# Two sets of small f32 buffers for the Strassen-like units, and two subtractions moved to VectorE, in a fused pooled-attention and SiLU-MLP kernel

## The chip, the cores and the metric

The kernel runs on one core of one Trainium2 chip. The metric is the device time of one execution in microseconds. Beside it stands a profile of one execution, whose span (first to last instruction) is about 2 us shorter than the time.

## The reference

Attention with keys and values pooled over 8 positions, then a two-layer MLP with SiLU over all tokens:

```python
k_p = k.reshape(B, H, Sp, pool, D).mean(axis=3)      # B, H, S, D = 8, 8, 576, 64; pool = 8, Sp = 72
v_p = v.reshape(B, H, Sp, pool, D).mean(axis=3)
scores = scale * np.matmul(q, k_p.transpose(0, 1, 3, 2))
attn = softmax(scores)
x = (attn @ v_p).transpose(0, 2, 1, 3).reshape(4608, 512)
h = x @ w_in                                          # 512 -> 2048
out = (h * sigmoid(h)) @ w_out                        # 2048 -> 512, float32
```

## The kernel before

The 4608 tokens are worked in nine tiles of 512 (`t` = 0 to 8). While tile `t` goes through the MLP, the attention of batch `t + 1` (576 tokens) is computed between its matmuls, so that its output `xT` is there for the tiles that follow. An order written out by hand sets what stands behind what on each engine; no scheduler moves it. Tiles 0 to 2 use a list of "fillers" with due places (`up`, `down`, `down_quarters`). Tiles 3 to 8 use `run`, which walks through the string `PROGRAM`, one token at a time.

**Matrix products in seven parts.** Most of both MLP products is done in Strassen's way: a 2x2 block product takes seven block products instead of eight, in return for sums before and after. In the first layer a *unit* is a set of four 128-row groups of the hidden layer; there are four unit sets, A, B, C, E (numbers 0, 1, 2, 3). The seven products of a unit go into three PSUM banks P, Q, R, which later products add to:

- product 2 into P, then ScalarE copies P to `r_sb` (line 506);
- product 5 into Q, then VectorE: `rr_sb` = Q + `r_sb` (line 509);
- product 1 into R, then VectorE: `t_sb` = R - `rr_sb` (line 512);
- product 4 added to P and 3 to Q, and ScalarE's SiLU of each into `h_T`;
- product 7 added to P, VectorE: `c_sb[0]` = P + `t_sb` (line 521), and 6 added to Q, VectorE: `c_sb[1]` = Q + `t_sb` (line 524), and SiLU of both (tokens `h` or `a`, and `s`).

A token such as `E3` in `PROGRAM` means product 3 of unit set E. An addition to a bank must come after what reads the bank's earlier contents: E3 adds to Q, so it waits for the addition that makes `rr_sb` of E from Q. Each product of a unit is four matmuls of 256 columns. The four unit sets are interleaved in the order C, B, A, E, each starting before the one before it has ended, and all of them use the one `r_sb`, the one `rr_sb` and the one `t_sb`.

**The second layer** (`down_stages`, tokens `d40` to `d63`) is one more product in seven parts over halves of `h_T`; five of its left-hand sides are sums `h_sum` (line 610, tokens such as `h6l`: sum number 6, low half; `h6h`, high half). It uses the same `r_sb`, `rr_sb` and `t_sb`. Two corrections are tokens of their own, on GpSimd (POOL):

- `u1`: `rr_sb` -= `o_sb[1]` left half (after product 2 has been copied there);
- `u2`: `rr_sb` -= `o_sb[0]` right half (after product 5 has been copied there).

Then `t_sb` = R + `rr_sb` (line 727) and the two last outputs (lines 729 and 733), each followed by its store. In the last tile, the end of `PROGRAM` is replaced by `L0` and `L1`: products 1, 7 and 6 are done for column half 0 with their additions and stores, and then for column half 1 (`columns`), so that less is left after the last matmul.

**Attention.** `scores` computes a visit's scores for a third of a batch and ScalarE's exponentials into `es`; `denominators` sums them with a matmul and makes the reciprocal `rec` by a logarithm into `lnd` and an exponential; `numerators` multiplies with the pooled values and writes `xT`. The third visit's numerators come in the next tile (token `npp`), except for the last batch. These small tiles come from a pool that hands out its buffers in turn; a new user of a buffer waits for the last reader of the one before.

Of the kernel before, what the change touches and what calls it, by code (L numbers as in the profile page):

```python
# [27 lines left out]
FP32 = mybir.dt.float32  # L28
FP32R = mybir.dt.float32r
BF16 = mybir.dt.bfloat16  # L30
# [6 lines left out]
def kernel(  # L37
# [9 lines left out]
    nc = tc.nc  # L47
# [3 lines left out]
    SP = S // POOL  # L51
# [9 lines left out]
    KQ, NQ, CQ = KG // 2, NTT // 2, d_model // 2  # L61
# [8 lines left out]
    VW = max(HS, 2 * S // 3)  # L70
# [11 lines left out]
    singles = ctx.enter_context(tc.tile_pool(name="singles", bufs=1))  # L82
    big = ctx.enter_context(tc.tile_pool(name="big", bufs=1))
    mid = ctx.enter_context(tc.tile_pool(name="mid", bufs=2))
# [22 lines left out]
        n: singles.tile([128, KQ, NQ], BF16, name=f"h_sum{n}") for n in (1, 2, 5, 6, 7)  # L107
    }
    o_sb = [singles.tile([128, 2, d_model], FP32, name=f"o_sb{n}") for n in range(2)]
    r_sb = singles.tile([128, 2, CQ], FP32, name="r_sb")  # L110
    rr_sb = singles.tile([128, 2, CQ], FP32, name="rr_sb")
    t_sb = singles.tile([128, 2, CQ], FP32, name="t_sb")
    xT = singles.tile([128, KF, NX], BF16, name="xT")

    w_sum1 = [
# [217 lines left out]
    def scores(b, segs):  # L333
        st = batches[b]
        w = width(segs)
        sc = [ps_tile([128, 512], FP32, "at", "sc_ps")[:SP, :w] for s in range(4)]
        for g, i0, i1, cs in seg_cols(segs):
            for c in range(2):
                for s in range(4):
                    rows = slice(32 * s, 32 * (s + 1))  # L340
                    nc.tensor.matmul(  # L341
                        sc[s][:, cs],
                        lhsT=kz[b % 2][rows, g, c, :],
                        rhs=st["qT"][rows, g, i0:i1, :, c],
                        start=(c == 0), stop=(c == 1),
                    )
        es = mid.tile([SP, 4, VW], BF16, tag="es", bufs=4, name="es")[:, :, :w]
        for s in range(4):
            nc.scalar.activation(es[:, s, :], sc[s], func=AF.Exp, scale=score_scale)  # L349
        st["es", segs] = es  # L350


    def denominators(b, segs, on_dve=False):
        st = batches[b]
        w = width(segs)
        es = st["es", segs]
        den_ps = ps_tile([128, 512], FP32, "at", "den_ps")
        for s in range(4):
            nc.tensor.matmul(  # L359
                den_ps[32 * s : 32 * (s + 1), :w],  # L360
                lhsT=ones, rhs=es[:, s, :], start=True, stop=True,
            )
        rec = mid.tile([128, VW], FP32, tag="rec", bufs=4, name="rec")[:, :w]
        if on_dve:
            nc.vector.reciprocal(rec, den_ps[:, :w])
        else:
            lnd = mid.tile([128, VW], FP32, tag="lnd", name="lnd")[:, :w]
            nc.scalar.activation(lnd, den_ps[:, :w], func=AF.Ln)  # L368
            nc.scalar.activation(rec, lnd, func=AF.Exp, scale=-1.0)
        st["rec", segs] = rec  # L370
# [107 lines left out]
    def unit_stages(t, step):  # L478
        ps = {}

        def product(y, n, bank, first):
            if first:
                tag = "mm" if bank == "R" else "at"
                ps[y, bank] = ps_tile([128, 2, NQ], FP32, tag, f"u_ps{bank}")
            w, x = unit_weights(y, n), unit_x(t, n)
            for u in range(2):
                next(step)
                for kk in range(2):
                    nc.tensor.matmul(  # L489
                        ps[y, bank][:, u, :], lhsT=w[:, kk, 128 * u : 128 * (u + 1)],  # L490
                        rhs=x[:, kk, :], start=first and u == 0 and kk == 0,
                        stop=kk == 1, skip_group_check=True,
                    )

        def hidden(y, i, j, src):
            g = UNITS[y][i]
            nc.scalar.activation(  # L497
                h_T[:, g : g + 2, j * NQ : (j + 1) * NQ], src, func=AF.Silu
            )

        tt = nc.vector.tensor_tensor

        def stage(y, n):
            if n == "2":
                product(y, 2, "P", True)
                nc.scalar.copy(r_sb, ps[y, "P"])  # L506
            elif n == "5":
                product(y, 5, "Q", True)
                tt(out=rr_sb, in0=ps[y, "Q"], in1=r_sb, op=ALU.add)  # L509
            elif n == "1":  # L510
                product(y, 1, "R", True)
                tt(out=t_sb, in0=ps[y, "R"], in1=rr_sb, op=ALU.subtract)  # L512
            elif n == "4":
                product(y, 4, "P", False)
                hidden(y, 1, 0, ps[y, "P"])
            elif n == "3":
                product(y, 3, "Q", False)
                hidden(y, 0, 1, ps[y, "Q"])
            elif n == "7":
                product(y, 7, "P", False)  # L520
                tt(out=c_sb[0], in0=ps[y, "P"], in1=t_sb, op=ALU.add)  # L521
            elif n == "6":
                product(y, 6, "Q", False)
                tt(out=c_sb[1], in0=ps[y, "Q"], in1=t_sb, op=ALU.add)  # L524
            elif n == "h":
                hidden(y, 0, 0, c_sb[0])
            else:
                hidden(y, 1, 1, c_sb[1])

        return stage  # L530
# [106 lines left out]
    def down_quarters(t, fillers, last=False):  # L637
        step = spread(fillers, 7 * 2 * KQ)
        ps = {
            n: ps_tile([128, 2, CQ], FP32, "mm", f"o_ps{n}") for n in "PQR"  # L640
        }
        bank = {2: "P", 5: "Q", 1: "R", 4: "P", 3: "Q", 7: "P", 6: "Q"}
        begun = set()

        def product(n, k0, k1, cs=(0, 1)):
            b = bank[n]
            for kt in range(k0, k1):
                for c in cs:
                    next(step)
                    nc.tensor.matmul(  # L650
                        ps[b][:, c, :], lhsT=left(n, kt, c), rhs=W_OUT[n][:, kt, :],
                        start=b not in begun,
                        stop=kt == k1 - 1, skip_group_check=True,
                    )
                    begun.add(b)

        add, sub = ALU.add, ALU.subtract
        tt = nc.vector.tensor_tensor
        KA = KQ // 2
        product(2, KA, KQ)  # L660
        product(5, KA, KQ)
        product(2, 0, KA)
        nc.scalar.copy(r_sb, ps["P"])
        product(5, 0, KA)
        tt(out=rr_sb, in0=ps["Q"], in1=r_sb, op=add)
        for cc in ((0,), (1,)) if last else ((0, 1),):
            cs = slice(cc[0], cc[-1] + 1)
            product(1, 0, KQ, cc)
            tt(out=t_sb[:, cs], in0=ps["R"][:, cs], in1=rr_sb[:, cs], op=sub)
            product(4, 0, KQ, cc)  # L670
            nc.scalar.copy(o_sb[1][:, cs, LO], ps["P"][:, cs])
            tail = last and cc == (1,)
            if tail:
                store(t, 3, LO, (nc.gpsimd,))
            product(3, 0, KQ, cc)
            nc.vector.tensor_copy(out=o_sb[0][:, cs, HI], in_=ps["Q"][:, cs])
            if tail:
                store(t, 1, HI)
            product(7, 0, KQ, cc)
            tt(out=o_sb[0][:, cs, LO], in0=ps["P"][:, cs], in1=t_sb[:, cs], op=add)  # L680
            for c in cc:
                store(t, c, LO if tail else FULL, (nc.scalar if tail else nc.sync,))
            product(6, 0, KQ, cc)
            tt(out=o_sb[1][:, cs, HI], in0=ps["Q"][:, cs], in1=t_sb[:, cs], op=add)
            for c in cc:
                if tail:
                    store(t, 3, HI, both)
                else:
                    store(t, 2 + c, FULL, (nc.gpsimd if last else nc.sync,))
        for _ in step:  # L690
            pass


    def down_stages(t, last):
        ps = {}
        bank = {2: "P", 5: "Q", 1: "R", 4: "P", 3: "Q", 7: "P", 6: "Q"}
        begun = set()
        add, sub = ALU.add, ALU.subtract
        tt = nc.vector.tensor_tensor

# [39 lines left out]
        def part_of(tok):  # L740
            if tok == "o":
                return after(6)
            n = int(tok[1])
            if tok[0] == "u":
                src = o_sb[1][:, :, LO] if n == 1 else o_sb[0][:, :, HI]
                nc.gpsimd.tensor_tensor(out=rr_sb, in0=rr_sb, in1=src, op=sub)  # L746
                return
            if not ps:
                for b in "PQR":
# [1 line left out]
            i = int(tok[2])  # L751
# [20 lines left out]
    def run(t):  # L772
# [7 lines left out]
        if last:  # L780
            i = toks.index("d10")
            sums = [x for x in toks[i:] if x[0] in "hu"]
            toks = toks[:i] + sums + ["L0", "L1"]
        toks = [x for x in toks if attn or x not in attn_toks]
        if a == B - 1:
            toks.insert(1 + max(toks.index("de2"), toks.index("nu1"), toks.index("o")), "nu2")
# [311 lines left out]
```

## Time and profile before

Time: 280.79 us, median of 3 runs (280.5 to 281.09). The profiled execution's span is 278.9 us; the granted TensorE clock was 0.999 of full speed.

| engine | busy us | share of the span |
|---|---|---|
| TensorE, matmuls (PE) | 271.2 | 97% |
| TensorE, weight loads (PEld) | 208.9 | 75% |
| VectorE (DVE) | 242.5 | 87% |
| ScalarE (ACT) | 190.8 | 68% |
| GpSimd (POOL) | 117.8 | 42% |

Rows of the page that touch the change, in the page's words: `L509 DVE TENSOR_TENSOR rr_sb<-u_psQ,r_sb` x29, 690 ns each; `L512 DVE TENSOR_TENSOR t_sb<-u_psR,rr_sb` x29, 687 ns; `L506 ACT COPY r_sb<-u_psP` x29, 585 ns; `L746 POOL TENSOR_TENSOR rr_sb<-rr_sb,o_sb` x12, 1709 ns; `L349 ACT ACTIVATE es<-sc_ps` x100, 471 ns.

How to read the lines: the first time is microseconds from the start of the span, the second a duration. "out<-in" names what is written and read, and "x4" means that four equal instructions are merged. Brackets at the end give how long the engine had been idle before, and what ended that wait. Matmuls overlap: four of them show 0.60 us, but the next four start 0.44 us after their start. In a table by windows the columns are the length of the window, busy time and count of PE, PEld, DVE, ACT and POOL, the granted clock, the DMA share and GB/s. The chain of waits follows the work that ended last back from the last instruction, and lists it in order of time; "issue" in it is time for which the profile shows no wait.

### The profile page before, as it was taken

The numbers are of one execution on the slowest core, as the hardware profiler recorded it, in microseconds if no ns is written. First come the engines' busy times: TensorE is split into PE (matmuls) and PEld (weight loads), VectorE is DVE, ScalarE is ACT, GpSimd is POOL, SyncE is SP. The second block draws the span as 40 slices with busy tenths as digits, with TensorE's granted clock in tenths as the row PEclk, the third lists the DMA queues.
The fourth block names the chain that finished last, engine by engine and source line by source line (L and its number), as shares of the span: only waits on it lengthen the run. The fifth ranks groups of instructions, "written<-read, shape, count | busy, mean of one in ns | idle before, by whom it ended". The sixth has DMA issues, their size and how long they took to land.

```text
span 278.9 us, 7359 instructions
## 1 busy us (share of the span) xinstructions
PE 271.2 (97%) x2923; PEld 208.9 (75%) x2933; DVE 242.5 (87%) x449; ACT 190.8 (68%) x373; POOL 117.8 (42%) x116
## 2 busy tenths in 40 slices
PE   8999999999999999999999999999999999999975
PEld 4458444576878678887888788877887788888864
DVE  4985777788998979998999899989999889998993
ACT  1788766468677956878677977797779858308700
POOL 8745217242158331945394429972811300130050
PEclk9999999999999999999999999999999999999999
DMA  7999999896759798569757825799510041014013
GB/s 214 280 257 242 206 324 179 237 161 120 159 73 229 196 139 161 140 161 129 134 112 191 133 43 131 184 104 144 138 26 0 2 114 40 2 31 121 1 38 115
DMA packets 31314, 37.73 MB, mean 135 GB/s; under 512 B 10352, under 2 KB 22256, under 8 KB 31280
## 3 DMA queue, kind: packets, MB, share of 16 engines
q0 software_dynamic: 23920, 27.03, 52.5%
q1 hardware_dynamic: 6928, 9.58, 12.5%
q10 hardware_dynamic: 432, 0.66, 0.7%
q8 instruction: 23, 0.38, 0.6%
q14 instruction: 11, 0.09, 0.1%
HBM read 36.70 MB, written 9.44 MB: 165 GB/s over the span
## 4 chain that ended last, share of the span: by engine, by line
PE 73%; DMA 12%; DVE 8%; issue 3%; POOL 2%; DVEq 0%; POOLq 0%
PE o_psQ L705 11%; PE o_psP L705 11%; PE u_psP L489 10%; PE u_psQ L489 9%; DMA w_in_sb<-in_moe_w_in_dram 6%; DMA w_out_sb<-in_moe_w_out_dram 6%; PE o_psQ L650 4%; PE o_psP L650 4%; PE hp_ps L542 4%; PE u_psR L489 4%; PE o_psR L705 4%; DVE t_sb L512 3%; PE sc_ps L341 3%; PE nu_ps L385 3%; PE o_ps L577 2%
## 5 line engine op out<-in xcount | busy, mean ns | idle before, releaser
L610 DVE TENSOR_TENSOR h_sum<-h_T 128x1024 bf16<-128x1024 bf16 (+1 forms) x78 | 57.4, 789 | 1.6 <-ACT h_T L548 1.0
L489 PEld LDWEIGHTS <-w_sum 128*128 128x128 bf16 x532 | 52.0, 98 | 7.2 <-issue 0.3
L705 PEld LDWEIGHTS <-h_sum 128*128 128x128 bf16 x480 | 45.6, 98 | 10.0 <-issue 2.3
L349 ACT ACTIVATE es<-sc_ps 72x384 bf16<-72x384 f32 (+1 forms) x100 | 39.1, 471 | 5.7 <-PE sc_ps L341 5.3
L497 ACT ACTIVATE h_T<-c_sb 128x512 bf16<-128x512 f32 x58 | 35.6, 627 | 8.7 <-DVE c_sb L521 8.4
L746 POOL TENSOR_TENSOR rr_sb<-rr_sb,o_sb 128x512 f32<-128x512 f32 x12 | 20.5, 1709 | 42.0 <-ACT o_sb L719 38.6
L506 ACT COPY r_sb<-u_psP 128x512 f32<-128x512 f32 x29 | 17.0, 585 | 22.6 <-PE u_psP L489 13.4
L542 PE MATMUL hp_ps<-xT,w_in_sb 128*128 128x512 bf16 (+2 forms) x151 | 25.9, 318 | 0.3
L489 PEld LDWEIGHTS <-w_in_sb 128*128 128x128 bf16 x232 | 22.5, 98 | 4.2 <-issue 1.3
L394 DVE TENSOR_TENSOR xT<-nu_ps,rec 128x384 bf16<-128x384 f32 (+1 forms) x50 | 23.9, 530 | 1.6 <-PE nu_ps L385 1.4
L509 DVE TENSOR_TENSOR rr_sb<-u_psQ,r_sb 128x512 f32<-128x512 f32 x29 | 20.0, 690 | 4.5 <-ACT r_sb L506 1.7
L191 POOL TENSOR_TENSOR raw<-raw 72x1024 f32<-72x1024 f32 x10 | 23.6, 2364 | 0.1
L512 DVE TENSOR_TENSOR t_sb<-u_psR,rr_sb 128x512 f32<-128x512 f32 x29 | 19.9, 687 | 3.0 <-PE u_psR L489 0.5
L548 ACT ACTIVATE h_T<-hp_ps 128x512 bf16<-128x512 f32 (+2 forms) x39 | 18.1, 476 | 5.8 <-PE hp_ps L542 4.8
L521 DVE TENSOR_TENSOR c_sb<-u_psP,t_sb 128x512 f32<-128x512 f32 x29 | 19.8, 683 | 1.9 <-PE u_psP L489 1.2
L524 DVE TENSOR_TENSOR c_sb<-u_psQ,t_sb 128x512 f32<-128x512 f32 x29 | 19.8, 684 | 1.3 <-PE u_psQ L489 1.1
L542 PEld LDWEIGHTS <-w_in_sb 128*128 128x128 bf16 x156 | 14.6, 98 | 8.5 <-issue 0.7
L705 PEld LDWEIGHTS <-h_T 128*128 128x128 bf16 x192 | 18.8, 98 | 2.2
L497 ACT ACTIVATE h_T<-u_psQ 128x512 bf16<-128x512 f32 x29 | 17.1, 590 | 3.3 <-PE u_psQ L489 3.1
L497 ACT ACTIVATE h_T<-u_psP 128x512 bf16<-128x512 f32 x29 | 17.4, 599 | 2.2 <-PE u_psP L489 2.1
L368 ACT ACTIVATE lnd<-den_ps 128x384 f32<-128x384 f32 (+1 forms) x23 | 11.2, 487 | 11.0 <-PE den_ps L359 11.0
L489 PE MATMUL u_psQ<-x_sum,w_in_sb 128*128 128x256 bf16 x116 | 17.5, 272 | 0.3
(104 smaller groups left out, 560.2 us busy)
## 6 DMA issues: line engine op xcount, KB each, us to landing
out_dram<-o_sb SPq DMA_DIRECT2D x128, 64.0 KB, 1.9
raw<-in_k_dram POOLq DMA_DIRECT2D x10, 576.0 KB, 8.0
raw<-in_v_dram POOLq DMA_DIRECT2D x10, 576.0 KB, 8.0
q_bf<-in_q_dram POOLq DMA_DIRECT2D x6, 576.0 KB, 10.7
w_in_sb<-in_moe_w_in_dram POOLq DMA_DIRECT2D x8, 256.0 KB, 8.3
w_out_sb<-in_moe_w_out_dram POOLq DMA_DIRECT2D x4, 512.0 KB, 13.5
raw<-in_v_dram POOLq DMA_DIRECT2D x2, 768.0 KB, 11.1
raw<-in_k_dram POOLq DMA_DIRECT2D x1, 768.0 KB, 10.2
```

The lines of the kernel that those rows point to most:

```text
L191: nc.gpsimd.tensor_add(out=raw[:, :, : 2 * D], in0=raw[:, :, : 2 * D], in1=raw[:, :, 2 * D :])
L349: nc.scalar.activation(es[:, s, :], sc[s], func=AF.Exp, scale=score_scale)
L394: nc.vector.tensor_mul(out=xT[:, 2 * g0 + c : 2 * (g0 + ng - 1) + c + 1 : 2, cols], in0=nu[c][:, :w].rearrange("r (g n) -> r g n", g=ng), ...
L489: nc.tensor.matmul(ps[y, bank][:, u, :], lhsT=w[:, kk, 128 * u : 128 * (u + 1)], rhs=x[:, kk, :], start=first and u == 0 and kk == 0, stop ...
L497: nc.scalar.activation(h_T[:, g : g + 2, j * NQ : (j + 1) * NQ], src, func=AF.Silu)
L509: tt(out=rr_sb, in0=ps[y, "Q"], in1=r_sb, op=ALU.add)
L512: tt(out=t_sb, in0=ps[y, "R"], in1=rr_sb, op=ALU.subtract)
L542: nc.tensor.matmul(hp_ps[:, r0:r1], lhsT=w_in_sb[:, kk, g * 128 : (g + 1) * 128], rhs=xT[:, kk, x0 : x0 + r1 - r0], start=(kk == 0), stop= ...
L610: nc.vector.tensor_tensor(out=h_sum[n][:, ks, :], in0=quarter(*a, ks), in1=quarter(*b, ks), op=op)
L650: nc.tensor.matmul(ps[b][:, c, :], lhsT=left(n, kt, c), rhs=W_OUT[n][:, kt, :], start=b not in begun, stop=kt == k1 - 1, skip_group_check= ...
L705: nc.tensor.matmul(ps[b][:, c, :], lhsT=left(n, kt, c), rhs=W_OUT[n][:, kt, :], start=b not in begun, stop=kt == k1 - 1, skip_group_check= ...
L746: nc.gpsimd.tensor_tensor(out=rr_sb, in0=rr_sb, in1=src, op=sub)
```

## The change

Units take turns with two sets of `r_sb`, `rr_sb` and `t_sb`, so that a unit's first sums need not wait until the unit before has read its own; the second layer uses set 0. The 6144 bytes a partition for this come from one buffer fewer of `es` (3 in place of 4), `rec` (3 in place of 4) and `lnd` (1 in place of 2). In the last tile the subtractions `u1` and `u2` go from GpSimd to VectorE, and stand behind the sums `h6h` and `h6l` in its order (before: `u1 h6h h6l u2` over the two engines; after: `h6h h6l u1 u2`, all on VectorE), so that these sums don't meet GpSimd's work.

The line with `r_sbs[0]` below stands once in `down_quarters` and once in `down_stages`.

```diff
-    r_sb = singles.tile([128, 2, CQ], FP32, name="r_sb")
-    rr_sb = singles.tile([128, 2, CQ], FP32, name="rr_sb")
-    t_sb = singles.tile([128, 2, CQ], FP32, name="t_sb")
+    r_sbs = [singles.tile([128, 2, CQ], FP32, name=f"r_sb{n}") for n in range(2)]
+    rr_sbs = [singles.tile([128, 2, CQ], FP32, name=f"rr_sb{n}") for n in range(2)]
+    t_sbs = [singles.tile([128, 2, CQ], FP32, name=f"t_sb{n}") for n in range(2)]
...
-        es = mid.tile([SP, 4, VW], BF16, tag="es", bufs=4, name="es")[:, :, :w]
+        es = mid.tile([SP, 4, VW], BF16, tag="es", bufs=3, name="es")[:, :, :w]
...
-        rec = mid.tile([128, VW], FP32, tag="rec", bufs=4, name="rec")[:, :w]
+        rec = mid.tile([128, VW], FP32, tag="rec", bufs=3, name="rec")[:, :w]
...
-            lnd = mid.tile([128, VW], FP32, tag="lnd", name="lnd")[:, :w]
+            lnd = mid.tile([128, VW], FP32, tag="lnd", bufs=1, name="lnd")[:, :w]
...
         def stage(y, n):
+            r_sb, rr_sb, t_sb = r_sbs[y % 2], rr_sbs[y % 2], t_sbs[y % 2]
...
+        r_sb, rr_sb, t_sb = r_sbs[0], rr_sbs[0], t_sbs[0]
...
                 src = o_sb[1][:, :, LO] if n == 1 else o_sb[0][:, :, HI]
-                nc.gpsimd.tensor_tensor(out=rr_sb, in0=rr_sb, in1=src, op=sub)
+                (nc.vector if last else nc.gpsimd).tensor_tensor(
+                    out=rr_sb, in0=rr_sb, in1=src, op=sub
+                )
...
             sums = [x for x in toks[i:] if x[0] in "hu"]
-            toks = toks[:i] + sums + ["L0", "L1"]
+            toks = toks[:i] + sorted(sums) + ["L0", "L1"]
```

More of the change, by code (lines that the diff above doesn't have):

```diff
@@ L697, in down_stages @@
         begun = set()
+        r_sb, rr_sb, t_sb = r_sbs[0], rr_sbs[0], t_sbs[0]
         add, sub = ALU.add, ALU.subtract
```

## The prediction, made before the change was run

> **What bounds the kernel now.** I read the page first, then busy time by windows, then the chain of waits in order of time for one unit stage, the timeline of VectorE and TensorE there, and last the timeline of the end.
>
> ```profile
> PE 271.2 (97%) x2923; PEld 208.9 (75%) x2933; DVE 242.5 (87%) x449; ACT 190.8 (68%) x373; POOL 117.8 (42%) x116
> 139.00:167.70 28.70, 28.65 (x339) 23.81 (x338) 26.52 (x47) 22.66 (x44) 15.36 (x12) 1.00 0.60 121
> 261.50:278.90 17.40, 12.62 (x114) 10.80 (x112) 12.78 (x21) 2.87 (x6) 4.13 (x4) 0.98 0.17 61
> ```
>
> The second and third lines are windows: length, then busy time of PE, PEld, DVE, ACT and POOL. In a middle tile TensorE is busy 28.65 of 28.70 us: only a hole in TensorE's row is worth anything there. At the end it is busy 12.62 of 17.40 us.
>
> TensorE's holes in tiles 3 to 8 show in the chain of waits. One unit stage, tile 8, in order of time (start, length, what):
>
> ```profile
> 254.96 0.45 PE u_psP L489 x4
> 255.42 0.70 DVE t_sb L512
> ...
> 257.45 0.69 DVE c_sb L524
> ...
> 258.24 0.70 DVE t_sb L512
> ...
> 259.07 0.70 DVE rr_sb L509
> 259.77 0.04 issue
> 259.81 0.60 PE u_psQ L489 x4
> ```
>
> The end leaves TensorE at 254.96, runs through VectorE's additions, and comes back at 259.81. The timeline shows what TensorE loses:
>
> ```profile
> 259.16 0.60 PE L489 MATMUL u_psQ<-x_sum,w_sum 128*128 128x256 bf16 x4
> 259.81 0.60 PE L489 MATMUL u_psQ<-x_sum,w_in_sb 128*128 128x256 bf16 x4
> 259.81 0.31 PEld L489 LDWEIGHTS <-w_in_sb 128*128 128x128 bf16 x3 [0.22 <-issue]
> ```
>
> Four matmuls start 0.44 us after the four before (258.72, 259.16), but E3 starts 0.65 later: a hole of 0.21 us. E3 adds to bank Q of unit set E, so it waits until `rr_sb` of E has read that bank (end of the 259.07 addition). The same step at 119.96, 148.62, 177.28, 205.94 and 235.15 in the chain makes six holes, 1.28 us. I find no other hole in the unit stages of these tiles except the short ones at changes of matmul shape, which wait for no vector.
>
> Why VectorE is late: its 128x512 f32 additions start 0.60 us apart when nothing orders them (256.25, 256.86, 257.45) and 0.79 to 0.83 apart when the later one needs the earlier one finished (257.45 to 258.24, 258.24 to 259.07). The 258.24 addition writes the `t_sb` that 257.45 reads; the 259.07 addition writes the `rr_sb` that 258.24 reads. Neither needs the other's value.
>
> The end of the last tile, timeline:
>
> ```profile
> 268.60 2.96 POOL L746 TENSOR_TENSOR rr_sb<-rr_sb,o_sb 128x512 f32<-128x512 f32 x2
> 268.74 0.69 DVE L723 COPY o_sb<-o_psQ 128x512 f32<-128x512 f32 x1 [0.16 <-PE o_psQ L705]
> 269.35 2.76 DVE L610 TENSOR_TENSOR h_sum<-h_T 128x1024 bf16<-128x1024 bf16 x2
> 269.41 1.04 PE L705 MATMUL o_psP<-w_sum,h_sum 128*128 128x256 bf16 x8
> 272.03 0.41 DVE L727 TENSOR_TENSOR t_sb<-o_psR,rr_sb 128x256 f32<-128x256 f32 x1
> 272.17 1.05 PE L705 MATMUL o_psQ<-w_sum,h_sum 128*128 128x256 bf16 x8 [1.72 <-DVE h_sum L610]
> 273.05 1.04 PE L705 MATMUL o_psR<-w_sum,h_sum 128*128 128x256 bf16 x8
> 275.87 0.42 DVE L733 TENSOR_TENSOR o_sb<-o_psQ,t_sb 128x256 f32<-128x256 f32 x1 [0.45 <-PE o_psQ L705]
> ```
>
> Two h sums take 2.76 us where four took 2.49 at 263.09, and product 6 waits for them.
>
> [...] POOL's subtractions run 268.60 to 271.56, and the pair of h sums ends only 0.55 us after that.
>
> **Part 1, fewer `es`, `rec`, `lnd`: nothing.** It pays for the new buffers: 3072 + 1536 + 1536 bytes a partition freed, 3 x 2048 used. Three exponential tiles are live at most: the third visit's are read by `npp` or its like before the next batch's third visit writes, and a slot comes round to the same visit of the next batch, a tile (28.7 us) later. In the first batch the fourth `scores` reuses a slot whose numerators stand before it in TensorE's own order. `lnd` is written and read by ScalarE alone, with other activations between two uses. High end: one exponential of 0.47 us held in each of five batches, 2.4 us; kept as a rival.
>
> **Part 2, two sets in the units.** Order is C, B, A, E, so neighbours get different sets (C, A: 0; B, E: 1), as does E against the tail (0). No instruction is added. Waits removed: `t_sb` write after the neighbour's c sums, `rr_sb` write after the neighbour's `t_sb`, and ScalarE's copy into `r_sb` after the neighbour's `rr_sb` addition (9.0 us in 13 waits by the page of waits; TensorE shows no hole for it). I rework tile 8, spacing 0.60 us, and at least 0.10 us after the matmuls' end (C6: 253.92 + 0.60, its addition 254.63):
> - t of B: 254.63 + 0.60 = 255.23 (was 255.42).
> - rr of A: A5 ends 255.83, so 255.93 (was 256.25).
> - c sums of B: 256.53; B6 ends 257.14, so 257.25.
> - t of A: 257.85. rr of E: E5 ends 258.45, so 258.55, ending 259.24.
> E3 could go at 259.60 and is free at 259.29. The hole closes with 0.31 us to spare, and even half the saving would close it. The next waits follow by the same step: E6 waits for a ScalarE activation that itself starts on E3's end, and the h sums are ready over 1 us before their product (263.78 against 264.94). So 6 x 0.21 = **1.28 us**. Tiles 1 and 2 have unit stages too, but their only comparable hole (62.20, some 0.17 us) waits for a ScalarE activation: nothing.
>
> **Part 3, the last tile.** It removes two POOL subtractions (1.28 and 1.60 us) and adds two to VectorE, behind the h sums. Relative to the old times:
> - Without POOL the h sums start 269.35 and 269.95 (0.60 apart, as at 263.09) and end at 270.64, so product 6 starts at 270.70 in place of 272.17.
> - The subtractions: the nearest row is the f32 SBUF addition of 128x512 in line 264, 676 ns, whose next, dependent one starts 0.72 us later (24.67, 25.39). Low end 0.68 (7.37, 8.05), high end 0.83, the dependent spacing of line 512. At 0.72: 270.55, 271.27, and `t_sb` at 271.99, ending 272.40. That is where it was (272.03): what the h sums gain, the subtractions take.
> - Queued behind: `t_sb`, and the R matmuls of column 1. In the trace the first matmul of each column-1 product carries a wait for VectorE, by its place for the reading of column 0 from the same bank. So R goes at 272.46, not at 270.70 + 0.87 = 271.57. Then P and Q at 0.875 each: 273.33 and 274.21. Last addition at + 1.07: 275.28, against 275.87.
> Gain **0.59 us**; at 0.68 it is 0.67, at 0.83 it is 0.37. The last store follows as before. POOL's own subtractions were on no other path in this tile.
>
> Sum: 280.79 - 1.28 - 0.59 = 278.92, say **278.9 us**.
>
> **The rivals.**
> - Column-1 matmuls do not wait for column 0's addition: then TensorE is the bound, products at 271.57, 272.45, 273.32, last addition 274.39, 1.48 us gained: 280.79 - 1.28 - 1.48 = 278.0. Against: those waits are in the trace.
> - The tail gives nothing, because subtractions on VectorE cost more than their 0.72: 279.5. For: `t_sb` has only 0.04 us in hand at my price.
> - The holes stay, another wait in place of `rr_sb` (bank Q or ScalarE): only the tail, 280.2. Against: E5 and `r_sb` of E (257.61) are ready before.
> - Slower: three exponential buffers hold `scores` in five batches, 2.4 us, less at most what is gained: 280.79 + 2.4 - 1.88 = 281.3. Against: the order of uses above.
>
> **How the numbers follow.** Forecast 0.66, full tail 0.08, no tail 0.10, holes stay 0.10, slower 0.06. The range 277.9 to 279.9 takes in the first three, 0.84, with the spread of the times before (0.3 us either way). Faster means below 280.23: the first three and half of the fourth, 0.89; same 0.05 from the fourth and a little of the last, 0.06; slower 0.05.
>
> **What would show it.** Right: E3 0.44 us after A6, the product in front of it, in every tile; ScalarE's `r_sb` no longer waiting for `rr_sb`; pairs of `c_sb` and `t_sb` 0.60 apart; in the last tile two h sums in about 1.3 us, and product 6 after a wait near 0.4 in place of 1.72, then a new hole near 0.9 before R. Wrong: the hole of 0.21 still there, ScalarE's `es` waiting for numerators, or `t_sb` of the last tile well past 272.

## The result and the profile after

The changed kernel takes 279.25 us (median of 6 runs, 279.04 to 279.42) against 280.99 for the kernel before, measured again beside it (median of 6, 280.5 to 281.7). The ratio is 0.9936 [0.9922, 0.995]: 1.74 us faster. The profiled spans are 277.0 us after and 278.9 before.

From the page of the kernel after, busy time by engine and the shares of the chain that ended last:

```profile
PE 270.7 (98%) x2923; PEld 209.1 (75%) x2933; DVE 241.2 (87%) x451; ACT 191.3 (69%) x373; POOL 114.3 (41%) x114
PE 82%; DMA 12%; POOL 2%; DVE 1%; issue 1%; DVEq 0%; POOLq 0%
```

VectorE has two instructions more (449 to 451) and GpSimd two fewer (116 to 114): the two subtractions. VectorE's share of the chain was 8% before (`PE 73%; DMA 12%; DVE 8%; issue 3%` on its page) and is now 1%: the chain no longer leaves TensorE for VectorE in front of E3.

The unit stage of tile 8, timeline of the kernel after. It runs 1.19 us earlier than before:

```profile
255.36 0.68 DVE L522 TENSOR_TENSOR c_sb<-u_psP,t_sb 128x512 f32<-128x512 f32 x1
...
256.06 0.69 DVE L525 TENSOR_TENSOR c_sb<-u_psQ,t_sb 128x512 f32<-128x512 f32 x1
...
256.67 0.68 DVE L513 TENSOR_TENSOR t_sb<-u_psR,rr_sb 128x512 f32<-128x512 f32 x1
...
257.37 0.69 DVE L510 TENSOR_TENSOR rr_sb<-u_psQ,r_sb 128x512 f32<-128x512 f32 x1
...
257.97 0.60 PE L489 MATMUL u_psQ<-x_sum,w_sum 128*128 128x256 bf16 x4
...
258.41 0.60 PE L489 MATMUL u_psQ<-x_sum,w_in_sb 128*128 128x256 bf16 x4
```

The reader is to see the last two lines: E3 (258.41) starts 0.44 us behind the product in front of it, where it was 0.65. The bank's reader is done well before: the addition that makes `rr_sb` of E ends at 258.06 (257.37 + 0.69), 0.35 us before E3. The `c_sb` to `t_sb` step is 0.61 (256.06 to 256.67), where it was 0.79. The same 0.43 or 0.44 stands in front of E3 in tiles 3 to 7 (at 119.60, 148.05, 176.50, 204.95 and 233.96 us). In the page of waits the 9.0 us of ScalarE's `r_sb` behind VectorE's `rr_sb` are gone.

The end of the last tile, timeline of the kernel after:

```profile
267.95 1.28 DVE L611 TENSOR_TENSOR h_sum<-h_T 128x1024 bf16<-128x1024 bf16 x2
...
269.15 1.41 DVE L749 TENSOR_TENSOR rr_sb<-rr_sb,o_sb 128x512 f32<-128x512 f32 x2
...
269.29 1.05 PE L708 MATMUL o_psQ<-w_sum,h_sum 128*128 128x256 bf16 x8 [0.24 <-DVE h_sum L611]
270.67 0.42 DVE L730 TENSOR_TENSOR t_sb<-o_psR,rr_sb 128x256 f32<-128x256 f32 x1
271.15 1.03 PE L708 MATMUL o_psR<-w_sum,h_sum 128*128 128x256 bf16 x8 [0.81 <-DVE t_sb L730]
...
273.96 0.42 DVE L736 TENSOR_TENSOR o_sb<-o_psQ,t_sb 128x256 f32<-128x256 f32 x1 [0.45 <-PE o_psQ L708]
```

The two h sums take 1.28 us in place of 2.76. Product 6 (269.29) waited 0.24 by the bracket in place of 1.72. A wait that was not there before now stands in front of R of column half 1 (271.15). From the start of R of column half 0 to the start of the last addition it was 7.33 us before (268.54 to 275.87), and is 6.82 now (267.14 to 273.96): 0.51 us gained. This stretch is called the tail below.

How the span's 1.9 us divide: the place of equal matmuls in the two traces moves from 0.15 us early (at 42.4 us, behind the last wait for a load in tile 0) to 1.40 early behind the last hole, in six steps of about 0.21, which makes 1.25; the tail gives 0.51; the 0.15 is the start of the kernel, where tile 0 waits for loads. In the traces below this start lies between 0.15 us earlier and 0.58 later than in the kernel before, so differences of medians below some 0.2 us are not read.

### The profile page after: what moved, and what is told of

Read it like the earlier page. It is cut to its first block, busy times and chain, and to the rows that moved or that the text cites. A ratio compares the mean times of both kernels' runs of the same rounds, so it can differ in the third digit from the quotient of the medians.

```text
span 277.0 us, 7372 instructions
## 1 busy us (share of the span) xinstructions
PE 270.7 (98%) x2923; PEld 209.1 (75%) x2933; DVE 241.2 (87%) x451; ACT 191.3 (69%) x373; POOL 114.3 (41%) x114
## 4 chain that ended last, share of the span: by engine, by line
PE 82%; DMA 12%; POOL 2%; DVE 1%; issue 1%; DVEq 0%; POOLq 0%
PE u_psP L489 14%; PE u_psQ L489 14%; PE o_psP L708 11%; PE o_psQ L708 11%; DMA w_in_sb<-in_moe_w_in_dram 7%; DMA w_out_sb<-in_moe_w_out_dram 6%; PE u_psR L489 5%; PE o_psQ L652 4%; PE o_psP L652 4%; PE o_psR L708 4%; PE hp_ps L543 4%; PE sc_ps L341 3%; PE nu_ps L385 3%; PE o_ps L578 2%; PE den_ps L359 2%; PE o_psR L652 1%
## 5 line engine op out<-in xcount | busy, mean ns | idle before, releaser
L611 DVE TENSOR_TENSOR h_sum<-h_T 128x1024 bf16<-128x1024 bf16 (+1 forms) x78 | 55.7, 765 | 1.8 <-ACT h_T L549 1.0
L749 POOL TENSOR_TENSOR rr_sb<-rr_sb,o_sb 128x512 f32<-128x512 f32 x10 | 16.9, 1687 | 42.3 <-ACT o_sb L722 36.5
L489 PE MATMUL u_psP<-x_sum,w_in_sb 128*128 128x256 bf16 x116 | 17.6, 273 | 0.0
```

Source lines behind the costliest of these rows:

```text
L489: nc.tensor.matmul(ps[y, bank][:, u, :], lhsT=w[:, kk, 128 * u : 128 * (u + 1)], rhs=x[:, kk, :], start=first and u == 0 and kk == 0, stop ...
L611: nc.vector.tensor_tensor(out=h_sum[n][:, ks, :], in0=quarter(*a, ks), in1=quarter(*b, ks), op=op)
```

## The experiments

**The theory**: six holes in front of E3 come from `rr_sb` and `t_sb` being shared by neighbouring units; two sets close them (1.28 us); the moved subtractions shorten the tail by about half a microsecond, because R of column half 1 stays behind `t_sb`; the smaller pools cost nothing. **Rivals**: the whole gain is the tail, or the smaller pools cost something, or it is ScalarE's wait for `rr_sb` (9.0 us) whose removal pays, or the order of the sums and not the engine of the subtractions.

### One half at a time

*The two sets without the tail* (`sets_only`): the change, with the subtractions on GpSimd and in the old order.

```diff
-                (nc.vector if last else nc.gpsimd).tensor_tensor(
-                    out=rr_sb, in0=rr_sb, in1=src, op=sub
-                )
+                nc.gpsimd.tensor_tensor(out=rr_sb, in0=rr_sb, in1=src, op=sub)
...
-            toks = toks[:i] + sorted(sums) + ["L0", "L1"]
+            toks = toks[:i] + sums + ["L0", "L1"]
```

> Two sets and fewer buffers, the last tile's subtractions on GpSimd in the old order. Theory (the holes before E3 are one part of the gain, the end another, and they add): 1.28 us less than the kernel before, ratio 0.9954; no hole before E3 in tiles 3 to 8, and product 6 of column half 0 still waits 1.7 us in the last tile. Rival (the two parts hide each other: with the holes gone the end waits for something that does not move): under 0.6 us less.

Measured: 279.73 us against 280.81, ratio 0.9957 [0.9942, 0.9971], 1.08 us gained. None of the six holes is left; product 6 waits 1.72 us, as before.

*The tail without the sets* (`tail_only`): the kernel before with those two hunks the other way round.

> The last tile's subtractions on VectorE behind the h sums, everything else as before. Theory: 0.5 to 0.6 us less than before, ratio 0.998; the six holes of 0.21 us stay, and the last tile shows a wait of some 0.3 us before product 6 and of 0.8 us before the second R. Rival (the end is worth more on its own, TensorE not being held by column half 0): 1.4 us less.

Measured: 280.35 us, ratio 0.9983 [0.9976, 0.9991], 0.46 us gained. All six holes are there (in tile 8, 259.10 to 259.75), and the tail is the same 6.82 us as with the whole change (268.48 to 275.30). The parts add: 1.08 + 0.46 = 1.54 us against 1.74, with intervals of about 0.4 us on the first and the last.

*The smaller pools alone* (`fewer_bufs`): the kernel before with `es` 3, `rec` 3 and `lnd` 1.

> Only es 3, rec 3 and lnd 1 buffers; one set, old end. Theory: the same time as before, within 0.2%, and no wait of es, rec or lnd for an older reader. Rival (some of the change's gain is eaten by scores that wait for a buffer): 0.3 to 2.4 us more.

Measured: 281.33 us, ratio 1.0019 [1.0012, 1.0025]: 0.52 us slower, which the theory did not have. Nothing waits for a buffer: ScalarE's `es` waits for scores 8 times, 5.3 us in all, in both kernels. What differs is one addition in tile 7, timeline of `fewer_bufs`, VectorE and then TensorE:

```profile
231.21 0.69 DVE L512 TENSOR_TENSOR t_sb<-u_psR,rr_sb 128x512 f32<-128x512 f32 x1
232.39 0.69 DVE L509 TENSOR_TENSOR rr_sb<-u_psQ,r_sb 128x512 f32<-128x512 f32 x1 [0.48 <-ACT h_T L497]
```

```profile
235.04 0.60 PE L489 MATMUL u_psQ<-x_sum,w_sum 128*128 128x256 bf16 x4
235.95 0.60 PE L489 MATMUL u_psQ<-x_sum,w_in_sb 128*128 128x256 bf16 x4 [0.31 <-DVE rr_sb L509]
```

`rr_sb` of A starts 1.18 us behind the addition in front of it, where it was 0.83 before (230.76, 231.59). The hole in front of E3 grows from 0.21 to 0.47 us (0.91 less the 0.44 of four matmuls). With 0.09 lost two products earlier, TensorE loses 0.35 us here. The name in the bracket misleads: nothing that the addition reads or overwrites was late. In VectorE's row (its instructions in order, waits among them) the wait in front of the addition stands at 231.94, 0.45 us before the start, against 0.10 in the kernel before (231.49 to 231.59). The remaining 0.17 us of the median lies within the spread of the start; whether the fewer buffers move the start too is not shown.

*The subtractions before the sums, both on VectorE* (`u_first`): the change with `sorted(sums)` replaced by `sums`, so `u1 h6h h6l u2`.

> The change with the last tile's tokens in the old order u1, h6h, h6l, u2, all on VectorE. Theory (what counts is that GpSimd no longer works beside the h sums, not that the subtractions stand behind them): as fast as the change, to 0.2 us less, because the h sums fill the gap between the two dependent subtractions; product 6 starts 0.6 us later, but R of column half 1, which waits for t_sb, does not. Rival (the order is what pays): 0.5 us more than the change.

Measured: 279.28 us, ratio 0.994 [0.9928, 0.9952], the same as the change. Product 6 starts 0.60 us later within the tail (2.75 us behind R of half 0, against 2.15), and still the last addition comes 0.13 us sooner (6.69 us against 6.82, 267.54 to 274.23): product 6 has time to spare, since R behind it waits for `t_sb` in either order (`t_sb` ends at 271.36 and R starts at 271.42; in the change 271.09 and 271.15). What pays is the engine, not the order.

### Which of the three buffers

Each is `sets_only` with one buffer alternating and the other two shared; for `only_rr`:

```diff
-            r_sb, rr_sb, t_sb = r_sbs[y % 2], rr_sbs[y % 2], t_sbs[y % 2]
+            r_sb, rr_sb, t_sb = r_sbs[0], rr_sbs[y % 2], t_sbs[0]
```

> Of the three buffers only r_sb has two, the end as before. Theory (VectorE's spacing sets E3; ScalarE's wait for r_sb is off the path): the six holes of 0.21 us stay, time as before; ScalarE no longer waits for rr_sb. Rival (the wait of ScalarE's copy into r_sb delays the chain): the holes close, 1.3 us less.

> Only rr_sb has two, the end as before. Theory: VectorE gains about 0.2 us twice between the t of B and the rr of E; more than the hole, so the six holes close and the time is 1.28 us less, as with all three. Rival (the pairs are needed together): holes of 0.1 us or more stay, under 0.7 us less.

> Only t_sb has two, the end as before. Theory: VectorE gains about 0.2 us twice (t of B, t of A), more than the hole, so the six holes close, 1.28 us less. Rival (the pairs are needed together, or rr_sb alone counts): holes stay, under 0.7 us less.

| kernel | us (before: 280.9) | ratio | step to E3 in tile 8 |
|---|---|---|---|
| `only_r` | 281.37 | 1.0018 [1.0011, 1.0024] | 0.65 |
| `only_rr` | 279.71 | 0.9955 [0.994, 0.9969] | 0.43 |
| `only_t` | 279.89 | 0.9962 [0.9948, 0.9977] | 0.44 |

The last column, in the timeline of `only_rr`:

```profile
258.48 0.60 PE L489 MATMUL u_psQ<-x_sum,w_sum 128*128 128x256 bf16 x4
258.91 0.60 PE L489 MATMUL u_psQ<-x_sum,w_in_sb 128*128 128x256 bf16 x4
```

Two `r_sb` alone take ScalarE's waits for `rr_sb` away and gain nothing; the kernel is as slow as `fewer_bufs`, whose pools it has. Two `rr_sb`, or two `t_sb`, close the holes alone: either takes two waits of about 0.2 us each out of VectorE's row in front of E3 (those of `rr_sb` of A and E, or those of `t_sb` of B and A), and the hole was 0.21. In tile 8, from the addition in front of `t_sb` of B to `rr_sb` of E, VectorE takes 4.44 us in the kernel before (254.63 to 259.07), 4.02 in `only_rr`, 4.04 in `only_t`, and 3.93 with all three buffers doubled. In tile 7 0.04 us of the hole stays with two `rr_sb` alone. With two `t_sb` alone one hole of 0.17 us stays, in tile 7 (234.07 to 234.68), where the addition that starts late in `fewer_bufs` has no slack left to hide in.

### What made the smaller pools cost something

> Of the fewer buffers only es 3 and lnd 1; rec keeps four. VectorE then has as many instructions as in the kernel before. Theory (fewer buffers cost nothing by themselves; the 0.35 us lost in tile 7 come from one more wait instruction in VectorE's row, which puts the rr_sb addition of unit A at place 576, a multiple of 64): no late start in tile 7, hole before E3 there 0.21 us, and at least 0.35 us less than with all three cut. Rival (the buffers themselves cost it): the hole of 0.47 us in tile 7 stays.

`es_lnd` is the kernel before with `es` 3 and `lnd` 1, and `rec` left at 4. Measured: 280.83 us, ratio 0.9994 [0.9985, 1.0003]. Its timeline of VectorE in tile 7 shows the step of before, 0.82:

```profile
230.74 0.69 DVE L512 TENSOR_TENSOR t_sb<-u_psR,rr_sb 128x512 f32<-128x512 f32 x1
231.56 0.69 DVE L509 TENSOR_TENSOR rr_sb<-u_psQ,r_sb 128x512 f32<-128x512 f32 x1
```

So it is `rec`. One `rec` fewer gives VectorE one wait instruction more, at a reciprocal ahead of the tiles, and moves all that follows one place on. `dve_plus_one` leaves the pools alone and adds one unrelated small instruction at the start, on a tile that is there already:

```diff
+    nc.vector.memset(gate, 0.0)
```

> The kernel before with one more VectorE instruction at the start, a memset of 128x1 elements; no buffer is changed. Theory (place in VectorE's row): the rr_sb addition of unit A in tile 7 starts 0.35 us after its waits are met, the hole before E3 there grows from 0.21 to some 0.47 us, and the time is 0.35 us more than before, ratio 1.0013. Rival (the fewer buffers cause it): nothing changes, ratio 1.000.

Measured: 281.27 us against 280.91, ratio 1.001 [1.0, 1.002]. The time alone leaves it open whether that is slower; the trace of `dve_plus_one` has the same late start:

```profile
230.99 0.69 DVE L512 TENSOR_TENSOR t_sb<-u_psR,rr_sb 128x512 f32<-128x512 f32 x1
232.18 0.69 DVE L509 TENSOR_TENSOR rr_sb<-u_psQ,r_sb 128x512 f32<-128x512 f32 x1 [0.50 <-ACT h_T L497]
```

The step is 1.19, and the hole in front of E3 in tile 7 is 0.47 again (234.83 to 235.74). What the pools cost is a place in VectorE's row, not a buffer. In the changed kernel this addition is late too (its waits met at 230.23, start 230.65), but with two sets it has slack, and E3 in tile 7 follows its predecessor by 0.44 us (233.52 to 233.96).

### A version that beats both

The new wait in front of R of column half 1 belongs to a row of VectorE that begins with a copy of Q, and ends at `t_sb`. `tail_act` gives that copy to ScalarE in the last tile and writes the order out by hand:

```diff
-                nc.vector.tensor_copy(out=o_sb[0][:, :, HI], in_=ps["Q"])
+                copy = nc.scalar.copy if last else nc.vector.tensor_copy
+                copy(out=o_sb[0][:, :, HI], in_=ps["Q"])
...
-            i = toks.index("d10")
-            sums = [x for x in toks[i:] if x[0] in "hu"]
-            toks = toks[:i] + sorted(sums) + ["L0", "L1"]
+            i = toks.index("d53")
+            toks = toks[:i] + ["u1", "h6h", "h6l", "d53", "u2", "L0", "L1"]
```

> The change, and in the last tile: the copy of Q to o_sb on ScalarE, and VectorE's u1, h6h, h6l in front of product 5's last matmuls, u2 behind its copy. Theory (the end is VectorE's work in a row up to t_sb, which R of column half 1 waits for): t_sb ends some 1.1 us earlier, product 6 waits under 0.1 us and R under 0.4, time 1.0 us less than the change. Rival (the end is bound by stores [...]): under 0.3 us less.

Measured: 278.13 us, ratio 0.9896 [0.9879, 0.9912], 1.1 us less than the change. In its timeline product 6 has no hole, and R (0.87 of matmuls, then 0.24 more) has little left (the copy and the order were not tried apart):

```profile
269.21 1.04 PE L708 MATMUL o_psQ<-w_sum,h_sum 128*128 128x256 bf16 x8
270.32 1.03 PE L708 MATMUL o_psR<-w_sum,h_sum 128*128 128x256 bf16 x8
```

The tail is 5.68 us (267.46 to 273.14) against 6.82.

`tail_act_R` adds a bank of its own (called S) for product 1 of column half 1, so that it no longer waits until `t_sb` of half 0 has read R:

```diff
+                    p = "S" if last and b == "R" and c else b
...
+                r = ps["S" if tail else "R"]
...
+                if last:
+                    ps["S"] = ps_tile([128, 2, CQ], FP32, "at", "o_psS")
```

> The version with the copy on ScalarE, and product 1 of column half 1 in a PSUM bank of its own in the last tile. Theory (R waits for t_sb of column half 0 only because both halves lie in one bank): the remaining hole of 0.24 us before R goes, time 0.24 us less than without, some 1.35 us less than the change. Rival (R waits for something else, such as the h sums): no difference.

Measured: 277.85 us, ratio 0.9887 [0.9871, 0.9904]. Products 6, 1 and 7 follow one another without a hole in its timeline, 0.87 apart:

```profile
269.07 1.04 PE L709 MATMUL o_psQ<-w_sum,h_sum 128*128 128x256 bf16 x8
269.94 1.04 PE L709 MATMUL o_psS<-w_sum,h_sum 128*128 128x256 bf16 x8
270.82 1.04 PE L709 MATMUL o_psP<-w_sum,h_sum 128*128 128x256 bf16 x8
```

The tail is 5.45 us (267.32 to 272.77). The other 0.05 of the 0.28 us between the two medians is within the spread.

## Why the prediction was right

Predicted 278.9 us, measured 279.25; or, against the kernel before as measured beside it, 1.87 us predicted and 1.74 measured. By its own steps:

- **Two sets close the six holes, 1.28 us: right.** In the trace the holes sum to 1.25 us; `sets_only` gains 1.08, with 1.28 inside its interval (0.0029 to 0.0058 of 280.81, 0.8 to 1.6 us). The rework of tile 8 can be laid beside the trace by taking 1.19 us from its times: `t_sb` of A 257.85 becomes 256.66 (measured 256.67), `rr_sb` of E 258.55 becomes 257.36 (257.37). From the end of that addition to E3 the rework had 0.36 us (259.24 to 259.60), and it is 0.35. That half the saving would do was right too, as `only_rr` and `only_t` show. So was that ScalarE's 9.0 us of waiting hide nothing, as `only_r` shows.
- **The fewer pool buffers cost nothing: right for the change, and not right alone.** No buffer waits anywhere, as argued. But `rec` 3 moves VectorE's row by one place, and in the kernel before that costs 0.35 us in the trace (`fewer_bufs`, `dve_plus_one`). The prediction counted the uses of the buffers and put the wait instruction that one `rec` fewer brings at nothing. In the changed kernel the slack made by part 2 takes the delay up, which was not foreseen.
- **The tail, 0.59 us: right in its mechanism, 0.08 too large.** Product 6 was to start after a hole near 0.4, and has one of 0.41 (268.01 to 269.29, less 0.87 of matmuls). R was to wait for `t_sb` with a new hole near 0.9; it is 0.99 (269.29 to 271.15, less 0.87). The mis-sized term is the last of the two dependent steps at 0.72. The chain of waits of the kernel after shows both:

```profile
269.23 0.61 DVE rr_sb L749
...
269.87 0.70 DVE rr_sb L749
...
270.67 0.44 DVE t_sb L730
...
271.15 1.03 PE o_psR L708 x8
```

Measured from the start of the first subtraction on VectorE's row (269.15) the second is 0.72 later, as priced. From the second to `t_sb` it is 0.80 (269.87 to 270.67). `t_sb` reads a PSUM bank, and its nearest row was line 512's, also a dependent addition that reads PSUM, at 0.83: the end of the range that was kept for the worst case. 0.59 less 0.08 is the 0.51 found.
- **Column half 1 waits: right, and shown by taking the wait away.** The rival with the whole tail gain needed R not to wait for `t_sb`. In the change R starts 0.06 us after `t_sb` of half 0 ends (271.09, 271.15), and in `tail_act` 0.05 us after (270.27, 270.32), with 0.24 us of hole left. With its own bank in `tail_act_R` product 1 starts at 269.94, without a hole, 0.19 us before that `t_sb` ends (270.13). S is another bank and also another buffer of the program; the run does not say for which of the two the wait was set.
- **GpSimd's subtractions lengthen the h sums: right.** Without them the two sums take 1.28 us, with them 2.76. In the trace of before each sum ends 0.55 to 0.56 us after one of the subtractions does (269.88 and 270.44, 271.56 and 272.11). Why the two go together is not shown.

Left open: 0.13 us between prediction and measured gain is smaller than the interval, and the start of the kernel moves by more than that from trace to trace.

## What to carry to other kernels

When a repeating hole on the bound engine ends behind a chain of additions on another, look for steps in that chain that only wait for a buffer to be read: it is enough to remove what makes up the hole (here either two of four waits), and waits with a large total may be worth nothing (here 9.0 us on ScalarE). Price a dependent step by the row with the same kinds of operands (in this tail 0.72 us between two SBUF subtractions, 0.80 into an addition that reads PSUM), not by the nearest name. Before work is moved to shorten a tail, follow the wait that takes over: here giving one copy to ScalarE, which had been idle for 1.16 us, with the sums in another order, and one product a bank of its own gained 1.4 us on top of the 0.5 of the move.

## What the runs showed that was not expected

- One more instruction far ahead in VectorE's row delayed an addition in tile 7 by 0.35 us. It comes at place 576 of that row when waits and other non-computing instructions are counted, and at 575 in the kernels without the delay. From its wait instruction to its start it took 0.42 to 0.46 us in the kernels with `rec` 3 and in `dve_plus_one`, and about 0.1 in the kernel before, `tail_only` and `es_lnd`. The same shows at place 192 in the three kernels without the delay at 576: there the `rr_sb` addition of tile 2 (85.07 us in the kernel before) starts 0.40 to 0.42 us after the end of its wait, against 0.12 in the others, where it comes at place 193. TensorE loses nothing by it: its groups of four matmuls start 0.43 or 0.44 us apart there (84.89 to 86.64 us in the kernel before). 192 and 576 are multiples of 64, but so is 128, where in the same three kernels an addition starts 0.04 us after the end of its wait. So 64 alone is not the rule, and what the engine does at these places stays open.
- A wait on the engine's own earlier work is not free on VectorE even where only a buffer's reuse is at stake: the same addition starts 0.60 to 0.61 us after the one in front of it without such a wait, and 0.79 to 0.83 with it (`t_sb` behind `c_sb` in tile 8: 0.79 in the kernel before, 257.45 to 258.24, and 0.61 in the change, 256.06 to 256.67). For these additions it costs about 0.2 us.
